# A fused attention and two expert layers on one core: second logits by column groups, both openers rearranged

## The chip, the cores and the metric

The kernel runs on one core of one Trainium2 chip, in one launch, on fp32 inputs and outputs. The metric is the device time of a run in microseconds. Before the change three runs gave 1098.56 to 1105.1, with a median of 1103.73. One execution was recorded by the hardware profiler; its own time is in the table of the section on the profile.

## The reference

Three stages run one after the other, on 3072 rows of 512 columns.

```python
# 1: attention, 4 batches x 8 heads x 768 rows x 64 columns
keep = (pos[None, :] < n_sink) | ((rel >= 0) & (rel < window))
a = softmax(where(keep, scale * q @ k.T, -1e9))
x = rows(a @ v)                                   # 3072 x 512
# 2: layer 1, 8 experts, each row goes to the expert with the largest logit
logits = x @ w_gate
out[mask] = gate_w[mask] * (relu(x[mask] @ w1[e]) @ w2[e])     # 512 -> 1024 -> 512
# 3: layer 2, the same, with a bias that depends on the row's modality
logits = x @ moe2_w_gate + modality_bias[modality_id]
out[mask] = gate_w[mask] * (relu(x[mask] @ w1[e]) @ w2[e])
```

The rows of a layer are sorted by expert on the chip, so that an expert's matmuls see its own rows alone.

## The kernel before

**Stages.** The attention takes the first 271 us: 96 units of 128 query rows of a pair of heads. While it runs, the routing of the first layer is computed for the batches that are done. Layer 1 follows as 15 blocks of 256 rows after an opener that holds block 0; layer 2 has the same form, an opener at about 714 us and 14 blocks.

**A block.** A block multiplies 256 gathered rows with one expert's `w1` (`h_products`, line 1016, TensorE tiles `hp`), keeps relu of that in a high part (`hh`, ScalarE, line 1031) and a low part (`hl`, VectorE, line 1032), and multiplies with `w2` (`y_products`, line 1025). Its second 128 rows are skipped at run time when there are none, so blocks take about 26.6 or 21.8 us. Weights come by SyncE's DMA into eight raw tiles, four of `w1` and four of `w2` (`piece`, lines 1207 and 1209); ScalarE casts each to a high part (line 1222), and VectorE or GpSimd subtracts that to get a low part (line 1225, called "low" here, numbered 0 to 7). A block prepares the weights of the next. In layer 1, lows 0 to 6 of a block are VectorE's and low 7 is GpSimd's. The rows of the next block are gathered by GpSimd (line 1230), turned by TensorE (line 1236, tiles `xp`), and split into high (line 1239, ScalarE) and low (line 1243, VectorE).

**Routing of layer 2.** Every layer-1 block also routes the rows that the block before it has put out (`Pending.route`): the rows are turned (line 1286), copied by ScalarE (line 1289), multiplied with the gate (line 1296, the "second logits"; 8 matmuls, one of 128 rows by 8 columns for each of two row tiles and four chunks of 128 columns). VectorE takes maximum and one-hot from that (lines 1325, 797 to 808), TensorE sums counts (line 817, "the prefix"), VectorE works out places and masks (lines 823 to 840), and TensorE adds them to a table (line 847).

**The openers.** Layer 1's opener (`Experts.open`) starts when the attention's last outputs are out (a branch of the instruction stream, line 742, lies between). It has the last routing of layer 1 in it, and its rows and weights are from a guess of which expert comes first. Layer 2's opener is the same code after the last routing of layer 2 (line 1366 on).

**What sets the order.** The order of each engine's instructions is fixed in the program: `Schedule.order` (line 424 on) is a list scheduler with a cost for each operation. Whenever an engine is free, it takes the ready operation with the least `late`; an operation with a larger `late` still starts when nothing else is ready on that engine. On the chip each engine works its list in order and waits for semaphores.

**Late blocks.** From layer-1 block 10 on, SyncE issues two conditional DMAs for each raw tile, one with this layer's weights and one with those of layer 2's opener (`block_load`); which of them moves data is known only at run time.

Of the kernel before, what the change touches and what calls it, by code (L numbers as in the profile page):

```python
# [74 lines left out]
class Kernel:  # L75
# [163 lines left out]
    def sink_keep(self, u):  # L239
        self.nc.gpsimd.tensor_copy(self.sp[u.pair % 2][:, u.i - 2], self.p[u.n % 4][:, :, 128:KEYS])  # L240

# [219 lines left out]
STEP = 2.05  # L461
START = {'DVE': 1.3, 'Pool': 2.0, 'SP': 9.0, 'ACT': 1.0}


class Attention:
# [20 lines left out]
    def misc(self, n):  # L486
        kk, mo, add = self.kk, self.kk.mo, lambda *args, **kw: self.add(MISC, *args, first=STEP * n, **kw)
        if n == 0:
            tmp = [("xt", 0, hp, i) for hp in range(2) for i in range(6)]
            add("DVE", 1.7, kk.masks_first, [], [("mask", 0), ("mask", 1), *tmp], late=-9)  # L490
            add("Pool", 2.8, kk.masks_window, [], [("mask", 2)], late=-9)
            add("DVE", 0.8, kk.masks_rest, [("mask", 2)], ["additive", *tmp], late=-8)
            held = [("xt", 1, hp, i) for hp in range(4) for i in range(6)]
            j = self.small()
            add("DVE", 0.4, kk.const_narrow, held, ["narrow"], late=8)
            add("DVE", 0.1, kk.mod_float, held, ["modf"], late=8)
            add("PE", 0.1, lambda: kk.mod_turn(j), [*held, "modf"], [("m", j)], late=8)
            add("DVE", 0.1, kk.mod_copy, [("m", j)], ["rowmod"], late=8)
# [14 lines left out]
    def unit(self, u):  # L513
# [7 lines left out]
        if i >= 2:  # L521
            add("Pool", 0.3, lambda: kk.sink_keep(u), [("p", n % 4)], [("sp", j, i)])
        add("PE", 0.26 * nk, lambda: kk.fast_turn(u), [("p", n % 4)], [("t", n % 2)], late=TURN_AT)
# [185 lines left out]
def attention(kk, mo, late, early):  # L709
# [147 lines left out]

OPEN_ENGINES = [["Pool", "DVE", "Pool", "Pool"] + ["Pool"] * 4, ["DVE", "Pool", "DVE", "Pool"] + ["Pool"] * 4]
OPEN_W = [2.3, 2.3]
# [7 lines left out]
class Experts:  # L867
# [124 lines left out]

    def rows_in(self, add, j, late, after=()):

        for t in range(2):
            add("PE", 0.45, lambda t=t: self.x_turn(t, t), [("xrow", t), *after], [("t", t)], late=late + 2 * PART * t)
            add("ACT", 0.55, lambda t=t: self.x_high(t), [("t", t)], ["xs", ("xh", t)], late=late + 2 * PART * t)
            add("DVE", 0.7, lambda t=t: self.x_low(t, j), [("t", t), ("xh", t), ("xrow", t)], ["xs", ("xl", t), ("rec", j)], late=late + 2 * PART * t)

# [50 lines left out]
    def open(self, router, s, then=None, w1=True, rows=True):  # L1050
# [9 lines left out]
        if rows:  # L1060
            self.rows_in(add, 0, -20)
        if not self.first:
# [22 lines left out]
    def block(self, b):  # L1085
# [127 lines left out]

    def block_load(self, m, late=False):

        ex, new, end = self.begins
        self.piece(self.w1, self.w2, ex, m, new > 0)
        if late:
            self.piece(self.io["moe2_w1"], self.io["moe2_w2"], self.opener, m, end > 0)

# [11 lines left out]

    def x_turn(self, t, turn=None):
        self.xp[t] = self.kk.bank("t", [128, 4, 128], "xp", turn)
        for c in range(4):
            self.nc.tensor.transpose(self.xp[t][:, c], self.xrow[:, t, 128 * c:128 * c + 128], self.kk.ident)  # L1236
# [23 lines left out]
class Pending:  # L1260


    def __init__(self, kk, mo):
        self.kk, self.nc, self.mo, self.yts = kk, kk.nc, mo, {}
        wk = mo.wk
        self.wg, self.yt = wk.tile([128, 4, E], F32, name="wg2"), mo.yt
# [4 lines left out]
        self.lg, self.bias, self.b, self.nmod, self.ok = f("lg", 2, E), f("bias", 2, E), f("b", 2, E), f("nmod", 2), f("ok", 2)  # L1271
        self.si = f("si", 2, dt=I32)
        self.router = Router(kk, 2, lambda *sh, dt=F32: f(f"r{next(num)}", *sh, dt=dt), "2", 1)

    def prepare(self):
        nc, io, r = self.nc, self.kk.io, self.router
        nc.sync.dma_start(self.mb, io["moe2_modality_bias"].partition_broadcast(128))
        nc.sync.dma_start(self.wg, io["moe2_w_gate"].rearrange("(c p) e -> p c e", p=128))

    def begin(self):  # L1280
        self.router.begin()

    def y_turn(self, y, t):
# [136 lines left out]
```

## Time and profile before

| | |
|---|---|
| runs: median (lowest to highest) | 1103.73 us (1098.56 to 1105.1) |
| profiled execution: its time, its span | 1100.99 us, 1098.8 us |
| mean granted TensorE clock of the profiled execution | 0.956 of full speed |
| TensorE busy | 1009.9 us, 92% |
| VectorE busy | 693.6 us, 63% |
| ScalarE busy | 551.2 us, 50% |
| GpSimd busy | 271.8 us, 25% |

The profiled execution's time and its span differ by 2.2 us, which lie outside the recorded instructions. "Busy" is the sum of an engine's instructions; an instruction that stands blocked counts as busy too. TensorE is nearly always at work in the blocks; the slices of the page in which it isn't are the first one (the start), those around 270 to 300 us (layer 1's opener), around 660 to 690 us (a late block) and around 715 to 745 us (layer 2's opener). Those four stretches, and one ordinary block, are read in the windows and timelines.

### The profile page before, as it was taken

The numbers are of one execution on the slowest core, as the hardware profiler recorded it, in microseconds if no ns is written. First come the engines' busy times: TensorE is split into PE (matmuls) and PEld (weight loads), VectorE is DVE, ScalarE is ACT, GpSimd is POOL, SyncE is SP. The second block draws the span as 40 slices with busy tenths as digits, with TensorE's granted clock in tenths as the row PEclk, the third lists the DMA queues.
The fourth block names the chain that finished last, engine by engine and source line by source line (L and its number), as shares of the span: only waits on it lengthen the run. The fifth ranks groups of instructions, "written<-read, shape, count | busy, mean of one in ns | idle before, by whom it ended". The sixth has DMA issues, their size and how long they took to land. (4 is left out here: it accounts for less than half of the span.)

```text
span 1098.8 us, 20203 instructions
## 1 busy us (share of the span) xinstructions
PE 1009.9 (92%) x6997; PEld 852.5 (78%) x6997; DVE 693.6 (63%) x1997; ACT 551.2 (50%) x1075; POOL 271.8 (25%) x269
## 2 busy tenths in 40 slices
PE   4999999987599999999999996948999999999995
PEld 2666666654499999999998995947989889898884
DVE  4565666574947877777777784664566555665554
ACT  2664656654245544445445562541555455554553
POOL 2111111113312422222223321351321112211121
PEclk9998999998599999999999997968999999999998
DMA  5355542351124142515133555211111421114610
GB/s 162 85 170 168 184 137 82 101 184 51 58 88 145 39 139 85 160 64 184 48 120 107 171 169 185 66 30 30 48 59 40 164 67 41 57 40 163 221 38 23
DMA packets 58462, 114.65 MB, mean 104 GB/s; under 512 B 10312, under 2 KB 22752, under 8 KB 58340
## 3 DMA queue, kind: packets, MB, share of 16 engines
q1 hardware_dynamic: 45860, 76.13, 20.9%
q0 software_dynamic: 11904, 36.31, 10.3%
q8 instruction: 61, 1.00, 0.4%
q10 hardware_dynamic: 576, 0.72, 0.2%
q14 instruction: 61, 0.50, 0.1%
HBM read 205.32 MB, written 28.92 MB: 213 GB/s over the span
## 5 line engine op out<-in xcount | busy, mean ns | idle before, releaser
L1025 PE MATMUL y<-w,hh 128*128 128x512 f32 x880 | 283.1, 403 | 0.0
L1225 DVE TENSOR_TENSOR w<-raw,w 128x1024 fp32r<-128x1024 f32 x161 | 192.4, 1217 | 76.0 <-ACT w L1222 75.3
L1016 PE MATMUL hp<-xs,first_w 128*128 128x256 f32 x1632 | 209.8, 285 | 1.7 <-DVE hl L1032 1.2
L1016 PEld LDWEIGHTS hp<-xs,first_w 128*128 128x128 f32 x1632 | 201.8, 191 | 6.7 <-DVE hl L1032 2.4
L1222 ACT CAST w<-raw 128x1024 fp32r<-128x1024 f32 x184 | 184.2, 1063 | 14.2 <-DMA raw<-in_moe_w_dram 11.5
L1016 PE MATMUL hp<-xs,w 128*128 128x256 f32 x1344 | 174.7, 287 | 12.3 <-DVE hl L1032 10.4
L1016 PEld LDWEIGHTS hp<-xs,w 128*128 128x128 f32 x1344 | 168.2, 193 | 16.9 <-DVE hl L1032 12.4
L1025 PEld LDWEIGHTS y<-w,hh 128*128 128x128 f32 x880 | 155.6, 189 | 25.8
L1025 PE MATMUL y<-w,hl 128*128 128x512 f32 x440 | 172.5, 392 | 0.0
L1031 ACT ACTIVATE hh<-hp 128x512 fp32r<-128x512 f32 x124 | 75.1, 606 | 131.2 <-PE hp L1016 122.7
L1225 POOL TENSOR_TENSOR w<-raw,w 128x1024 fp32r<-128x1024 f32 x23 | 60.1, 2622 | 207.8 <-ACT w L1222 207.7
L1225 DVE TENSOR_TENSOR first_w<-raw,first_w 128x1024 fp32r<-128x1024 f32 x59 | 70.3, 1220 | 64.5 <-ACT first_w L1222 64.0
L1239 ACT CAST xs<-xp 128x512 fp32r<-128x512 f32 x66 | 38.7, 586 | 142.3 <-PE xp L1236 140.5
L267 ACT ACTIVATE early<-early,late 128x272 f32<-128x272 f32 (+1 forms) x192 | 94.6, 496 | 23.4 <-DVE late L261 23.4
L1032 DVE SCALAR_TENSOR_TENSOR hl<-hp,hh 128x512 fp32r<-128x512 f32 x124 | 85.0, 686 | 30.1 <-ACT hh L1031 28.8
L261 DVE CUSTOM_DVE_ANT_0 early<-s,late 128x272 f32<-128x272 f32 (+1 forms) x192 | 72.7, 410 | 49.1 <-PE s L255 48.3
L1046 ACT ACTIVATE yrow<-y,rec 128x512 f32<-128x512 f32 x62 | 42.1, 688 | 122.0 <-PE y L1025 119.5
L1243 DVE TENSOR_TENSOR xs<-xp,xs 128x512 fp32r<-128x512 f32 x66 | 45.6, 691 | 85.7 <-ACT xs L1239 85.1
L1025 PEld LDWEIGHTS y<-w,hl 128*128 128x128 f32 x440 | 82.9, 188 | 19.1
L1256 POOL DMA_INDIRECT out_dram<-yrow,si x30 | 31.6, 1055 | 250.8 <-ACT yrow L1046 199.3
L255 PE MATMUL s<-early 64*128 64x272 f32 (+1 forms) x384 | 79.1, 444 | 11.7 <-DMA early<-in_kT_dram 9.7
L274 PE MATMUL t<-consts,early 128*128 128x128 f32 x352 | 62.4, 296 | 7.1 <-ACT early L267 4.5
(222 smaller groups left out, 1208.9 us busy)
## 6 DMA issues: line engine op xcount, KB each, us to landing
raw<-in_moe_w_dram SPq DMA_DIRECT2D x320, 512.0 KB
Y<-yrow SPq DMA_DIRECT2D x12, 514.0 KB
X<-late POOLq DMA_DIRECT2D x8, 771.0 KB, 4.5
early<-in_qT_dram SPq DMA_DIRECT2D x16, 384.0 KB
early<-in_kT_dram SPq DMA_DIRECT2D x16, 384.0 KB
early<-in_vN_dram SPq DMA_DIRECT2D x24, 256.0 KB
late<-in_vN_dram SPq DMA_DIRECT2D x64, 8.0 KB
late<-in_consts_dram ACTq DMA_DIRECT2D x1, 608.0 KB
```

The source lines that it names most:

```text
L255: self.nc.tensor.matmul(u.s[h][:, 0:u.keys], q[:, 128 * i:128 * i + 128], k.rearrange("p a s -> p (a s)")[:, KEYS * w:KEYS * w + u.keys], ...
L261: self.nc.vector.tensor_tensor_reduce(self.sc[u.n % 3][:, h, 0:n], u.s[h][:, 0:n], mask, -0.125, 3.0e38, ALU.add, ALU.min, accum_out=self. ...
L267: self.nc.scalar.activation(self.p[u.n % 4][:, h, 0:n], self.sc[u.n % 3][:, h, 0:n], AF.Exp, bias=self.nb[u.b % 2][:, u.i, g:g + 1], scale ...
L274: self.nc.tensor.transpose(u.t[:, kb, h], self.p[u.n % 4][:, h, KEYS * kb:KEYS * kb + 128], self.ident)
L1016: nc.tensor.matmul(hps[g][:, j], w[c][:, fs], xs[:, c, part], start=(c == 0 and w is whi and part == 0), stop=last)
L1025: nc.tensor.matmul(ys[t], a[:, f, ts], b[m][:, ws], start=start, stop=stop)
L1031: add("ACT", 0.6, lambda g=g, gs=gs: nc.scalar.activation(hh[:, gs], hps[g], AF.Relu), [("s", g % 2)], [("hh", g)], late=at - 3 + 2 * HALF ...
L1032: add("DVE", 0.7, lambda g=g, gs=gs: v.scalar_tensor_tensor(hl[:, gs], hps[g], 0.0, hh[:, gs].bitcast(F32), ALU.max, ALU.subtract), [("s", ...
L1046: add("ACT", 0.7, lambda t=t: nc.scalar.activation(y[:, t, 0:DM], ys[t], AF.Copy, scale=rec[:, 0, t:t + 1]), bank + ["rec"], [("out", t)], ...
L1222: self.nc.scalar.copy(self.hi[s][m], self.raw[m])
L1225: (eng or self.nc.gpsimd).tensor_tensor(self.lo[s][m], self.raw[m], self.hi[s][m].bitcast(F32), ALU.subtract)
L1243: v.tensor_tensor(self.xs[:, :, 1, t], self.xp[t], self.xs[:, :, 0, t].bitcast(F32), ALU.subtract)
```

## The change

1. **Second logits.** The 8 matmuls of `y_products` become 4 in column groups: the gate's 8 columns are the stationary side, both row tiles (256 rows) the moving side, and each chunk's result goes to its own 8 partitions (32c to 32c+7) of one bank. ScalarE copies the bank (`parts_copy`, 128 x 256), and two matmuls with a 0/1 matrix `sel` add the four groups and turn the result (`parts_sum`). The bank is cleared once, in `begin`.
2. **Openers' rows.** `rows_in` gets `early`: in the openers both turns come at once, into banks that are free there, ahead of the rest.
3. **Openers' lows.** All eight lows of each opener are VectorE's; 13 of them were GpSimd's (7 in layer 1's opener, 6 in layer 2's). Low 7 of the layer-1 blocks stays on GpSimd.
4. **Loads for the next layer.** `block_load` no longer issues the second DMA; `next_load` does, as an operation of its own with `late` 23.0 and up.
5. **Start and tail of the attention.** The masks and the first sink columns are written ahead of the branch into the fast attention instead of inside its schedule; four constants move from unit 0 to unit 10; the copies of sink columns for the last two pairs of heads (line 240) go to VectorE; the assumed start times of the engines change.

```diff
     def sink_keep(self, u):
-        self.nc.gpsimd.tensor_copy(self.sp[u.pair % 2][:, u.i - 2], self.p[u.n % 4][:, :, 128:KEYS])
+        (self.nc.vector if u.last else self.nc.gpsimd).tensor_copy(self.sp[u.pair % 2][:, u.i - 2], self.p[u.n % 4][:, :, 128:KEYS])
...
-START = {'DVE': 1.3, 'Pool': 2.0, 'SP': 9.0, 'ACT': 1.0}
+START = {'DVE': 0.5, 'Pool': 1.0, 'SP': 5.0}
...
-        if n == 0:
-            tmp = [("xt", 0, hp, i) for hp in range(2) for i in range(6)]
-            add("DVE", 1.7, kk.masks_first, [], [("mask", 0), ("mask", 1), *tmp], late=-9)
-            add("Pool", 2.8, kk.masks_window, [], [("mask", 2)], late=-9)
-            add("DVE", 0.8, kk.masks_rest, [("mask", 2)], ["additive", *tmp], late=-8)
+        if n == 10:
             held = [("xt", 1, hp, i) for hp in range(4) for i in range(6)]
...
     kk.mask_setup()
+    kk.masks_window()
+    kk.masks_first()
+    kk.masks_rest()
+    kk.k_sinks(0, nc.vector)
...
-OPEN_ENGINES = [["Pool", "DVE", "Pool", "Pool"] + ["Pool"] * 4, ["DVE", "Pool", "DVE", "Pool"] + ["Pool"] * 4]
+OPEN_ENGINES = [["DVE"] * 8] * 2
 LOW_ENGINES = [["DVE"] * 7 + ["Pool"], ["DVE"] * 8]
...
-    def rows_in(self, add, j, late, after=()):
+    def rows_in(self, add, j, late, after=(), early=False):
 
         for t in range(2):
-            add("PE", 0.45, lambda t=t: self.x_turn(t, t), [("xrow", t), *after], [("t", t)], late=late + 2 * PART * t)
...
+            keys = [("t", t)] if not early else [("o", x) for x in range(4)] if t else [("s", 2)]
+            add("PE", 0.5, lambda t=t: self.x_turn(t, early and (("o", 0) if t else ("s", 2))), [("xrow", t), *after], keys, late=late + 2 * PART * t)
...
-            self.rows_in(add, 0, -20)
+            self.rows_in(add, 0, -150, early=True)
...
-            add("SP", 0.3, lambda m=m: self.block_load(m, late), ["regs"], [("raw", m)], late=1.5 + 2.6 * m)
+            add("SP", 0.3, lambda m=m: self.block_load(m), ["regs"], [("raw", m)], late=1.5 + 2.6 * m)
+            if late:
+                add("SP", 0.3, lambda m=m: self.next_load(m), ["regs"], [("raw", m)], late=23.0 + 0.1 * m)
...
     def begin(self):
         self.router.begin()
+        self.nc.vector.memset(self.kk.bank("m", [128, 256], "lz", 2), 0.0)
...
     def y_products(self):
-        self.products = self.kk.bank("m", [128, 2, E], "lp", 2)
+
+        self.parts = self.kk.bank("m", [128, 256], "lp", 2)
+        for c in range(4):
+            self.nc.tensor.matmul(self.parts[32 * c:32 * c + E], self.wg[:, c], self.yt[:, :, 128 * c:128 * c + 128], start=True, stop=True)
+
+    def parts_copy(self):
+        self.nc.scalar.copy(self.yt[:, 0, 0:256], self.parts)
+
+    def parts_sum(self):
+        self.products = self.kk.bank("m", [128, 2, E], "lq", 2)
         for t in range(2):
-            x = grp(self.yt[:, t], 4)
-            for c in range(4):
-                self.nc.tensor.matmul(self.products[:, t], x[:, c], self.wg[:, c], start=c == 0, stop=c == 3)
+            self.nc.tensor.matmul(self.products[:, t], self.yt[:, 0, 128 * t:128 * t + 128], self.sel, start=True, stop=True)
...
-        add("PE", 1.75, self.y_products, [("yt", 0), ("yt", 1)], [("m", 2)], late=at + 3 * HALF - 0.1)
+        add("PE", 0.6, self.y_products, [("yt", 0), ("yt", 1)], [("m", 2)], late=at + 3 * HALF - 0.1)
+        add("ACT", 0.35, self.parts_copy, [("m", 2)], [("yt", 0)], late=at + 3 * HALF - 0.1)
+        add("PE", 0.45, self.parts_sum, [("yt", 0)], [("m", 2)], late=at + 3 * HALF - 0.1)
```

How this moves the instructions is shown at three places. The first is TensorE's list from the attention's end into layer 1's opener (`xn`, `lt` and `lg` are the last steps of layer 1's logits, `xp` the turned rows, `hp` the opener's first products). Before:

```order
L742 UNCONDITIONAL_BRANCH
L302 MATMUL xn<-consts,late 128x128 x4
L332 MATMUL lg<-consts,late 128x128 x3
L302 MATMUL xn<-consts,late 128x128 x8
L324 MATMUL lt<-late 32x384 x4
L817 LDWEIGHTS b_ltri
L817 MATMUL halves<-late,b_ltri 128x8
```

After the change:

```order
L742 UNCONDITIONAL_BRANCH
L1241 MATMUL xp<-consts,xrow 128x128 x8
L302 MATMUL xn<-consts,late 128x128 x4
L332 MATMUL lg<-consts,late 128x128 x3
L302 MATMUL xn<-consts,late 128x128 x8
L1017 MATMUL hp<-xs,first_w_123 128x256 x24
L324 MATMUL lt<-late 32x384 x4
```

Before, the turns and all 48 `hp` matmuls stand further down, the first `hp` behind the last table (lines 847 and 854). Now both turns stand first, and half of `hp` stands ahead of the last `lt`.

The second is VectorE's list in the middle of a layer-1 block (`raw_95` to `raw_98` are lows 3 to 6, `pd_lg` and `pd_r` the routing of layer 2, line 803 the one-hot). Before:

```order
L1032 SCALAR_TENSOR_TENSOR hl<-hp,hh 128x512
L1225 TENSOR_TENSOR w_9215<-raw_95,w_9215 128x1024
L1325 TENSOR_TENSOR pd_lg<-halves,pd_bias 128x16
L797 TENSOR_REDUCE pd_r_149<-pd_lg 128x2
L798 TENSOR_TENSOR pd_r_145<-pd_lg,pd_r_149 128x16
L1225 TENSOR_TENSOR w_9215<-raw_96,w_9215 128x1024
L800 SCALAR_TENSOR_TENSOR pd_r_148<-pd_r_145,consts 128x16
L801 TENSOR_REDUCE pd_r_150<-pd_r_148 128x2
L1225 TENSOR_TENSOR w_9215<-raw_97,w_9215 128x1024
L1032 SCALAR_TENSOR_TENSOR hl<-hp,hh 128x512
L802 TENSOR_REDUCE pd_r_151<-pd_r_146 128x2
L803 TENSOR_TENSOR pd_r_148<-consts,pd_r_150 128x16
```

After the change (lines 1229, 1033 and 1342 are what 1225, 1032 and 1325 were):

```order
L1229 TENSOR_TENSOR w_9204<-raw_96,w_9204 128x1024
L1229 TENSOR_TENSOR w_9204<-raw_97,w_9204 128x1024
L1033 SCALAR_TENSOR_TENSOR hl<-hp,hh 128x512
L1342 TENSOR_TENSOR pd_lg<-halves,pd_bias 128x16
L797 TENSOR_REDUCE pd_r_149<-pd_lg 128x2
L798 TENSOR_TENSOR pd_r_145<-pd_lg,pd_r_149 128x16
L1229 TENSOR_TENSOR w_9204<-raw_98,w_9204 128x1024
L1033 SCALAR_TENSOR_TENSOR hl<-hp,hh 128x512
L800 SCALAR_TENSOR_TENSOR pd_r_148<-pd_r_145,consts 128x16
L801 TENSOR_REDUCE pd_r_150<-pd_r_148 128x2
L802 TENSOR_REDUCE pd_r_151<-pd_r_146 128x2
L803 TENSOR_TENSOR pd_r_148<-consts,pd_r_150 128x16
```

The logits' first use has moved behind lows 4 and 5 and the second `hl`, and the steps of lines 800 to 803 behind low 6 and the third `hl`.

The third is SyncE's list at the head of a late block (`raw_92` and `raw_93` are raw tiles 0 and 1, `vi` and `gi` the experts' numbers). Before:

```order
L1152 TENSOR_LOAD vi
L1152 TENSOR_LOAD gi
L1207 ISA
L1207 DMA raw_92<-in_moe_w_dram 128x1024
L1207 ISA
L1207 DMA raw_92<-in_moe_w_dram 128x1024
L1207 ISA
L1207 DMA raw_93<-in_moe_w_dram 128x1024
```

After the change (line 1210 is what 1207 was):

```order
L1155 TENSOR_LOAD vi
L1155 TENSOR_LOAD gi
L1210 ISA
L1210 DMA raw_92<-in_moe_w_dram 128x1024
L1210 ISA
L1210 DMA raw_92<-in_moe_w_dram 128x1024
L1210 ISA
L1210 DMA raw_93<-in_moe_w_dram 128x1024
```

Each raw tile still has its two DMAs one right behind the other.

## Rows read from the trace of the kernel before

**Rows 1.** The page's busy time of each engine: us, share of the span, instructions.

```profile
PE 1009.9 (92%) x6997; PEld 852.5 (78%) x6997; DVE 693.6 (63%) x1997; ACT 551.2 (50%) x1075; POOL 271.8 (25%) x269
```

**Rows 2.** Windows: stretch, length, busy PE, PEld, DVE, ACT, POOL (instructions), PEclk, DMA.

```profile
271.10:296.60 25.50, 11.30 (x66) 7.70 (x66) 21.33 (x64) 6.19 (x11) 10.95 (x6) 0.57 0.17 64
...
296.60:321.00 24.40, 24.40 (x158) 22.27 (x157) 10.24 (x48) 4.25 (x7) 3.90 (x4) 0.96 0.16 44
...
529.40:556.00 26.60, 26.60 (x186) 24.33 (x185) 19.06 (x51) 13.37 (x19) 7.08 (x5) 1.00 0.12 41
...
653.00:693.20 40.20, 29.78 (x186) 27.12 (x187) 20.94 (x73) 13.88 (x20) 8.90 (x6) 0.83 0.61 200
...
714.40:768.30 53.90, 35.61 (x204) 32.11 (x205) 31.98 (x98) 16.20 (x23) 21.60 (x13) 0.75 0.11 30
```

**Rows 3.** Timeline, start: start, length, engine, line, operation, [idle before, releaser].

```profile
11.64 0.40 POOL L204 TENSOR_SCALAR late<-late 128x256 f32<-128x256 f32 x1
...
15.13 0.22 DVE L347 CAST late<-late 24x128 f32<-24x128 int32 x1 [1.51 <-DMA late<-in_moe_modality_id_dram]
...
16.57 0.28 DVE L261 CUSTOM_DVE_ANT_0 early<-s,late 128x128 f32<-128x128 f32 x1
```

**Rows 4.** Timeline of the attention's tail, DVE and PE.

```profile
259.76 1.18 DVE L1225 TENSOR_TENSOR first_w<-raw,first_w 128x1024 fp32r<-128x1024 f32 x1
...
263.44 0.33 PE L244 MATMUL halves<-consts,late 128*128 128x128 f32 x1 [2.42 <-POOL late L240]
```

**Rows 5.** Timeline of the first layer's opener: PE, DVE, POOL, PE.

```profile
273.38 0.63 PE L302 MATMUL xn<-consts,late 128*128 128x128 f32 x4 [2.29 <-issue]
...
281.26 5.43 DVE L825 TENSOR_TENSOR late<-late 128x24 f32<-128x24 f32 x1
...
281.98 4.65 POOL L1225 TENSOR_TENSOR w<-raw,w 128x1024 fp32r<-128x1024 f32 x2
...
295.02 1.72 PE L847 MATMUL tab<-late 128*96 128x256 bf16 x6 [3.48 <-DVE late L840]
```

**Rows 6.** Timeline of one block of the first layer: PE, POOL, DVE, PE.

```profile
534.54 1.85 PE L1296 MATMUL halves<-wg,yt 128*128 128x8 f32 x16
...
536.24 4.49 PE L1016 MATMUL hp<-xs,first_w 128*128 128x256 f32 x36
...
540.01 2.41 POOL L1225 TENSOR_TENSOR w<-raw,w 128x1024 fp32r<-128x1024 f32 x1 [13.39 <-ACT w L1222]
...
540.45 2.01 DVE L803 TENSOR_TENSOR pd_r<-consts,pd_r 128x16 f32<-128x16 f32 x1
...
544.10 0.18 PE L817 MATMUL halves<-pd_r,b_ltri 128*128 128x8 bf16 x1
...
545.03 0.62 PE L1025 MATMUL y<-w,hh 128*128 128x512 f32 x2
...
545.72 0.62 PE L1025 MATMUL y<-w,hh 128*128 128x512 f32 x2
```

**Rows 7.** Column groups in the attention (PE timeline); ACT's copies by line.

```profile
238.60 0.85 PE L324 MATMUL lt<-late 128*32 128x384 f32 x8
...
239.38 0.73 PE L255 MATMUL s<-early 64*128 64x272 f32 x4
...
L279 ACT COPY early<-t 128x256 f32<-128x256 f32 x15 | 5.6, 374 | 8.8 <-PE t L274 8.8
```

**Rows 8.** Timeline of the late blocks, SP's DMA issues and PE.

```profile
656.36 16.24 SPq L1209 DMA_DIRECT2D raw<-in_moe_w_dram  x8
...
674.93 1.44 PE L1016 MATMUL hp<-xs,w 128*128 128x256 f32 x5 [10.42 <-DVE hl L1032]
```

**Rows 9.** Timeline of the second layer's opener: POOL, DVE, PE.

```profile
736.89 6.96 POOL L1225 TENSOR_TENSOR w<-raw,w 128x1024 fp32r<-128x1024 f32 x3
...
736.19 7.69 DVE L828 TENSOR_SCALAR pd_r<-pd_r 128x2 int32<-128x2 int32 x1
...
745.15 1.21 PE L847 MATMUL tab<-pd_r,pd_r 128*96 128x256 bf16 x4 [8.24 <-DVE pd_r L840]
```

More of the change, by code (lines that the diff above doesn't have):

```diff
@@ L487, in misc @@
         kk, mo, add = self.kk, self.kk.mo, lambda *args, **kw: self.add(MISC, *args, first=STEP * n, **kw)
-        if n == 0:
-            tmp = [("xt", 0, hp, i) for hp in range(2) for i in range(6)]
-            add("DVE", 1.7, kk.masks_first, [], [("mask", 0), ("mask", 1), *tmp], late=-9)
-            add("Pool", 2.8, kk.masks_window, [], [("mask", 2)], late=-9)
-            add("DVE", 0.8, kk.masks_rest, [("mask", 2)], ["additive", *tmp], late=-8)
+        if n == 10:
             held = [("xt", 1, hp, i) for hp in range(4) for i in range(6)]
             j = self.small()
[L495 to L498, printed above, removed]
+            add("DVE", 0.4, kk.const_narrow, held, ["narrow"])
+            add("DVE", 0.1, kk.mod_float, held, ["modf"])
+            add("PE", 0.1, lambda: kk.mod_turn(j), [*held, "modf"], [("m", j)])
+            add("DVE", 0.1, kk.mod_copy, [("m", j)], ["rowmod"])
         if n == 14:
@@ L521, in unit @@
         if i >= 2:
-            add("Pool", 0.3, lambda: kk.sink_keep(u), [("p", n % 4)], [("sp", j, i)])
+            add("DVE" if u.last else "Pool", 0.25, lambda: kk.sink_keep(u), [("p", n % 4)], [("sp", j, i)])
         add("PE", 0.26 * nk, lambda: kk.fast_turn(u), [("p", n % 4)], [("t", n % 2)], late=TURN_AT)
@@ L617, in all @@
             u.b, u.hp = divmod(pair, H // 2)
+            u.last = pair >= pairs - 2
             u.i, u.n, u.pair, u.keys, u.copy = i, n, pair, WIDE if i else 128, "DVE" if COPY_DVE(n) else "ACT"
@@ L723, in attention @@
         kk.k_load(n)
-    kk.k_sinks(0, nc.vector)
     kk.wg1, kk.mod = late.take(4, 32), late.take(TILES)
@@ L991, in weights_in @@
         add(eng, 2.5 if eng == "Pool" else 1.27, lambda: self.low(s, m, self.nc.vector if eng == "DVE" else None), [("raw", m), ("hi", m)], [("lo", m), *reads], late=late, **kw)
-    def rows_in(self, add, j, late, after=()):
+    def rows_in(self, add, j, late, after=(), early=False):
         for t in range(2):
-            add("PE", 0.45, lambda t=t: self.x_turn(t, t), [("xrow", t), *after], [("t", t)], late=late + 2 * PART * t)
-            add("ACT", 0.55, lambda t=t: self.x_high(t), [("t", t)], ["xs", ("xh", t)], late=late + 2 * PART * t)
-            add("DVE", 0.7, lambda t=t: self.x_low(t, j), [("t", t), ("xh", t), ("xrow", t)], ["xs", ("xl", t), ("rec", j)], late=late + 2 * PART * t)
+            keys = [("t", t)] if not early else [("o", x) for x in range(4)] if t else [("s", 2)]
+            add("PE", 0.5, lambda t=t: self.x_turn(t, early and (("o", 0) if t else ("s", 2))), [("xrow", t), *after], keys, late=late + 2 * PART * t)
+            add("ACT", 0.55, lambda t=t: self.x_high(t), keys, ["xs", ("xh", t)], late=late + 2 * PART * t)
+            add("DVE", 0.7, lambda t=t: self.x_low(t, j), [*keys, ("xh", t), ("xrow", t)], ["xs", ("xl", t), ("rec", j)], late=late + 2 * PART * t)
     def rows_fetch(self, add, rows, late, reads=()):
@@ L1212, in block_registers, with block_load, next_load @@
         self.begins = self.load(self.vi[0:1, b], E - 1, engines=(mybir.EngineType.SP,))
[L1214 to L1219, printed above, removed]
+    def block_load(self, m):
+        self.piece(self.w1, self.w2, self.begins[0], m, self.begins[1] > 0)
+    def next_load(self, m):
+        self.piece(self.io["moe2_w1"], self.io["moe2_w2"], self.opener, m, self.begins[2] > 0)
     def high(self, s, m):
@@ L1231, in gather, with x_turn @@
                                               in_offset=bass.IndirectOffsetOnAxis(ap=rows[:, t:t + 1], axis=0))
-    def x_turn(self, t, turn=None):
-        self.xp[t] = self.kk.bank("t", [128, 4, 128], "xp", turn)
+    def x_turn(self, t, bank=None):
+        kind, turn = bank or ("t", t)
+        self.xp[t] = self.kk.bank(kind, [128, 4, 128], "xp", turn)
         for c in range(4):
@@ L1265, in __init__ @@
         wk = mo.wk
-        self.wg, self.yt = wk.tile([128, 4, E], F32, name="wg2"), mo.yt
+        self.wg, self.sel, self.yt = wk.tile([128, 4, E], F32, name="wg2"), wk.tile([128, E], F32, name="sel"), mo.yt
         self.mb = wk.tile([128, 2, E], F32, name="mb")
@@ L1270, in __init__ @@
         self.pay, self.pi = f("pay", 2, 2), f("pi", 2, 2, dt=I32)
-        self.lg, self.bias, self.b, self.nmod, self.ok = f("lg", 2, E), f("bias", 2, E), f("b", 2, E), f("nmod", 2), f("ok", 2)
+        self.lg, self.bias, self.nmod, self.ok = f("lg", 2, E), f("bias", 2, E), f("nmod", 2), f("ok", 2)
         self.si = f("si", 2, dt=I32)
         self.router = Router(kk, 2, lambda *sh, dt=F32: f(f"r{next(num)}", *sh, dt=dt), "2", 1)
+        self.b = self.router.b
     def prepare(self):
@@ L1278, in prepare @@
         nc.sync.dma_start(self.wg, io["moe2_w_gate"].rearrange("(c p) e -> p c e", p=128))
+        nc.vector.tensor_reduce(self.sel, self.kk.ident.rearrange("p (c e) -> p e c", c=4)[:, 0:E], AX.X, ALU.add)
     def begin(self):
         self.router.begin()
+        self.nc.vector.memset(self.kk.bank("m", [128, 256], "lz", 2), 0.0)
     def y_turn(self, y, t):
```

## The prediction

> **What bounds the kernel.** I read the page's busy times first. TensorE is busy for 1009.9 us, 92% of the span [rows 1], so about 89 us are not TensorE's work, and a change that takes little work off it can win only where it waits. The windows show where. An ordinary layer-1 block is full: TensorE is busy for 26.60 of 26.60 us [rows 2]. Layer 1's opener is not: between the attention's end at 271.1 and 296.6 TensorE works 11.30 of 25.50 us, while VectorE shows 21.33 and GpSimd 10.95; the stretch from 296.6 to 321.0 is full again [rows 2]. Layer 2's opener has 35.61 of 53.90, and one late block takes 40.20 us with 29.78 of work [rows 2]. The chain of waits reaches back only over the last blocks and tells nothing of these places, so I went on with the timelines of each.
>
> In the openers the reader is to see VectorE's tiny instructions stand for microseconds beside GpSimd's subtractions: line 825 (128x24) takes 5.43 us and ends when the two lows on GpSimd end, at 281.98 + 4.65 = 286.63 [rows 5]; line 828 (128x2) takes 7.69 beside three lows of 6.96 [rows 9]. They feed the masks, and TensorE waits 3.48 and 8.24 us for masks ahead of its tables [rows 5, 9].
>
> **Start.** The masks on GpSimd end at 11.64 + 0.40 = 12.04, but the first score on VectorE starts at 16.57 [rows 3]; between lies, among others, a cast that waited 1.51 us for the modality DMA [rows 3] and now comes ten units later. With the masks done ahead of the branch I put the first score at about 14: three small mask steps behind 12.04 and the read of the branch's flag. Gain 2.5; bounds 0 (if a load ends last) and 2.9.
>
> **Tail of the attention.** TensorE waits 2.42 us for GpSimd's copy of line 240, which stood behind two gathers [rows 4]. On VectorE it has two new lows of 1.18 ahead of it [rows 4], so the wait becomes 1.6 at worst: gain 0.8; bounds 0 and 2.4.
>
> **Layer 1's opener.** From 271.1 to the next block at 321.0 are 49.9 us, with 11.30 + 24.40 = 35.7 of TensorE's work [rows 2]. The branch's 2.29 [rows 5] stays, so 38.0 is the floor and 11.9 the most that can go. The turns now stand first and 24 `hp` ahead of the last logits, so products fill the waits of the routing. VectorE gets four lows, 4 x 1.18 = 4.7, but loses the blocked time of line 825 alone, 5.43 less some 0.2. What becomes late next is the gather of the next block's rows: it follows the last table, and fewer products are left behind the table to cover it. I allow 3 for that wait with its turn and copies, and take 9. Least: 5, line 825's time alone.
>
> **Layer-1 blocks.** The second logits' 16 records stand from 534.54 to the next product at 536.24, 1.70 us [rows 6]. Nearest to the column groups is line 324, 8 records of 384 columns, 238.60 to 239.38, 0.78 us [rows 7]; for 256 columns 0.52, between 0.26 (a third) and 0.78. The two sums are 4 records of the old kind, 4/16 of 1.70 = 0.43. Saving 1.70 - 0.95 = 0.75 a block, between 0.49 and 1.01.
>
> But the saving has to get past the prefix. The new ScalarE copy, 0.37 [rows 7], stands among the casts, the logits reach VectorE behind two more lows, and lines 800 to 803 stand behind low 6 and the third `hl`. TensorE started the prefix at 544.10 [rows 6]; it now comes 0.75 earlier but has one more step of `y` ahead of it, 545.72 - 545.03 = 0.69 [rows 6], so it asks at 544.04. When is the one-hot there? Line 803 waited in this block until GpSimd's low 7 ended (540.01 + 2.41 = 542.42; line 803 ended at 542.46) [rows 6]. With the copy low 7 can start at about 540.4. If VectorE's low 6 goes first (1.18, from about 540.2), GpSimd follows until 543.8, and six small steps of some 0.1 follow: 544.5, a wait of 0.46. If GpSimd goes first, 542.8 + low 6 + the third `hl` + the same steps give 545.3, a wait of 1.26. Without the change TensorE would have come to the same point at 544.10 + 0.69 = 544.79. So a block gains 0.3 or loses 0.5. I take 0.2, nearer to the first, since low 6's input is ready first. Ahead of the late blocks' wait a saving only lengthens that wait, so I count 12 of 15: 2.4.
>
> The Trainium skill ("SBUF — State Buffer", Who interferes with whom) says that a VectorE instruction with two SBUF inputs and a GpSimd instruction that reads SBUF exclude each other for a whole instruction, and that the one issued first blocks the other. By that rule alone the blocks give 12 x 0.3 = 3.6 and the sum falls by 1.2. The trace agrees in line 803; it disagrees in line 825, which was issued at 281.26, 0.72 ahead of GpSimd's lows, and lost all the same [rows 5].
>
> **Layer 2's opener.** The 8.24 us ahead of its tables [rows 9] are there because three lows on GpSimd held line 828; those lows are VectorE's now and none is left on GpSimd. VectorE was busy 31.98 of 53.90 us [rows 2], 7.5 of it blocked in line 828, so six lows of 1.18 (7.1) fit in their place. Gain 8.2; bounds 5 (the lows stand ahead of the masks) and 11 (some of the other idle of 53.90 - 35.61 = 18.3 goes too).
>
> **Loads for the next layer.** In the late blocks SyncE's 8 issues take 16.24 us, and TensorE waits 10.42 in the block from 653 [rows 8], which is 40.20 long where 26.60 is full [rows 2]. The change means to part the two loads of a raw tile, yet SyncE's list still has them in pairs: the second becomes ready right behind the first on an idle queue, and a larger `late` doesn't hold it back. So 0.
>
> **Sum.** 2.5 + 0.8 + 9 + 2.4 + 8.2 = 22.9 off the profiled execution's 1100.99 gives 1078.1. That execution is 2.7 below the runs' median of 1103.73, from which the sum gives 1080.8. I take 1079.
>
> **Rivals.**
>
> The logits' saving arrives in full, because VectorE keeps up and the prefix never waits: 12 x 0.75 = 9.0 instead of 2.4, 1072. For it: VectorE was busy only 19.06 of 26.60 us in a block [rows 2]. Against it: the chain above. Chance 0.15.
>
> GpSimd's low 7 goes first in every block: -0.5 x 12 = -6 instead of +2.4, 1087. For it: line 825 lost though issued first. Chance 0.14.
>
> The column groups don't overlap, so that the logits save nothing; then TensorE asks for the prefix at 544.8, waits 0 to 0.5, and the blocks give 0 to -6: 1081 to 1087. The row speaks against it: 8 records of 384 columns pass in 0.78, the switch into the groups and out of them included [rows 7]. Chance 0.05. The Trainium skill ("TensorEngine Tiling (Array Packing)", Key Properties) says that a change of tiling mode drains TensorE, which would take from the saving; the row has such a drain inside its 0.78 if there is one.
>
> VectorE becomes the bound in the openers: the lows stand ahead of the masks and the gains halve to 8.6 of 17.2: 1088. For it: 21.33 of 25.50 busy [rows 2]; against it: much of that was blocked time. Chance 0.13.
>
> The loads do come apart at run time, or the earlier start of their chain frees the late block: 40.20 - 26.60 = 13.6 more, 1065. Against it stands SyncE's list. Chance 0.06.
>
> On the other side: in every layer-1 block the prefix waits so long that it eats the rest, 20.5 us in 12 blocks, 1.7 each. That needs the one-hot at 544.79 + 1.7 = 546.5, when GpSimd is first and ScalarE's copy and casts come one cast later still; from 547.4 on (2.6 a block) the kernel is over 1% slower, 1112. Against it: two delays must meet in all blocks. Chance 0.04, half of it beyond 1%.
>
> The forecast keeps 0.43. The range takes in its own bounds and the rivals except the far ends: 1064 to 1091. About 1%, 11 us, is what a measurement of this kernel tells from no change. Faster by over that means below 1093 and holds in all cases but the last and the worst of the openers' and blocks' losses together: 0.89. Within it 0.09, slower 0.02.
>
> **What would show it.** In the changed kernel's profile: the first score near 14 us; no VectorE instruction of over 2 us in either opener and no GpSimd low there; `hp` of layer 1's opener within 12 us of the attention's end, and the next block some 41 us after it with a wait of 1 to 3 us for gathered rows; about 0.8 us less of wait at line 244; a second-logits group of about 0.5 us with sums of 0.4, and a wait of 0.4 to 1.3 at the prefix; no wait over 1 us ahead of layer 2's tables; a late block that still waits about 10 us for a load. I would be wrong first in the openers, if the gather chain after the last table is longer than the products that are left, or in the blocks, if the order of low 6 and low 7 goes the other way.

## The result and the profile after

The changed kernel takes 1072.38 us (median of four runs, 1070.82 to 1073.76) against 1103.91 (four runs, 1098.56 to 1105.1): a ratio of 0.9723, 95% interval 0.9688 to 0.9758. The forecast was 1079 with a range of 1064 to 1091. The profiled execution took 1072.99, 28.0 less than the one before.

The page's busy times answer to [rows 1]: TensorE works 16.5 us less, and GpSimd 34.

```profile
PE 993.4 (93%) x6933; PEld 823.2 (77%) x6933; DVE 688.9 (64%) x2020; ACT 555.6 (52%) x1091; POOL 237.9 (22%) x248
```

The windows answer to [rows 2] (stretch, length, busy PE, PEld, DVE, ACT, POOL, then PEclk, DMA share, GB/s): layer 1's opener up to the next block, one full block, a late block, and layer 2's opener up to the next block.

```profile
272.07:310.15 38.08, 31.80 (x222) 27.60 (x222) 26.06 (x106) 11.90 (x21) 3.61 (x4) 0.96 0.16 57
...
514.55:540.75 26.20, 26.20 (x183) 23.01 (x182) 18.87 (x51) 13.65 (x20) 7.35 (x5) 1.00 0.13 41
...
637.10:677.20 40.10, 29.90 (x181) 26.23 (x182) 20.91 (x73) 14.03 (x21) 8.29 (x7) 0.87 0.63 206
...
697.88:740.68 42.80, 30.76 (x199) 26.01 (x200) 26.52 (x101) 16.31 (x24) 8.78 (x7) 0.88 0.13 40
```

The reader is to see four lengths: 38.08 where 49.9 stood, 26.20 where 26.60 stood, 40.10 where 40.20 stood, and 42.80 where 53.90 stood. Full blocks took 26.60 and 26.74 in turn before, 26.67 on average, so one gains 0.47. The attention's end, however, is at 272.07 instead of 271.09. From these the difference of the two spans, 27.6, adds up: -1.0 to the attention's end, +11.8 in the first opener, +11.1 in the second, and +5.7 between the two, in layer 1's blocks.

The start and the attention, TensorE but for the first row and GpSimd's two (line 171 puts sink columns into the keys, line 240 keeps sink columns, and line 244 turns what line 240 has kept):

```profile
14.32 0.27 DVE L261 CUSTOM_DVE_ANT_0 early<-s,late 128x128 f32<-128x128 f32 x1
...
44.03 0.26 POOL L171 COPY early<-early 128x80 f32<-128x80 f32 x1 [4.12 <-PE t L274]
...
44.23 0.21 POOL L240 COPY late<-early 128x32 f32<-128x32 f32 x1
...
29.07 0.27 PE L244 MATMUL halves<-consts,late 128*128 128x128 f32 x1
...
44.49 0.33 PE L244 MATMUL halves<-consts,late 128*128 128x128 f32 x1 [0.60 <-POOL late L240]
...
49.61 0.49 PE L285 MATMUL o<-late 128*128 128x128 f32 x2 [0.50 <-ACT late L295]
...
54.63 0.48 PE L255 MATMUL s<-early 64*128 64x128 f32 x2 [0.43 <-DVE late L261]
...
56.79 0.27 PE L244 MATMUL halves<-consts,late 128*128 128x128 f32 x1
...
250.69 0.66 PE L274 MATMUL t<-consts,early 128*128 128x128 f32 x4 [2.71 <-DVE late L318]
...
263.57 0.47 PE L244 MATMUL halves<-consts,late 128*128 128x128 f32 x1 [0.64 <-DVE late L240]
...
274.22 1.06 PE L1241 MATMUL xp<-consts,xrow 128*128 128x128 f32 x8 [2.15 <-issue]
```

The first score comes 2.25 us earlier than in [rows 3], and the first of the halves steps (line 244) at 29.07 came at 29.55 before. Then waits follow, and the third halves step is at 56.79. The wait of [rows 4] at line 244 is 0.64 now, but 2.71 stand ahead of a turn at 250.69.

Layer 1's opener, TensorE, to the next block:

```profile
279.60 4.83 PE L1017 MATMUL hp<-xs,first_w 128*128 128x256 f32 x24
...
307.34 1.04 PE L1241 MATMUL xp<-consts,xrow 128*128 128x128 f32 x8
...
309.25 0.39 PE L1017 MATMUL hp<-xs,first_w 128*128 128x256 f32 x1 [0.87 <-ACT xs L1244]
...
310.15 1.57 PE L1017 MATMUL hp<-xs,first_w 128*128 128x256 f32 x11 [0.52 <-DVE xs L1248]
```

The first products start 7.5 us after the attention's end. Behind the last `y` stand the turns of the next block's rows and waits of 0.87 and 0.52: the exposed gather.

One layer-1 block, TensorE, VectorE and GpSimd, as in [rows 6]:

```profile
519.79 0.62 PE L1303 MATMUL halves<-yt,wg 128*8 128x256 f32 x8
...
520.34 3.06 PE L1017 MATMUL hp<-xs,first_w 128*128 128x256 f32 x24
...
523.24 0.51 PE L1311 MATMUL halves<-sel,yt 128*128 128x8 f32 x4
...
523.60 1.65 PE L1017 MATMUL hp<-xs,first_w 128*128 128x256 f32 x12
...
529.43 0.17 PE L817 MATMUL halves<-pd_r,b_ltri 128*128 128x8 bf16 x1
...
525.33 3.39 POOL L1229 TENSOR_TENSOR w<-raw,w 128x1024 fp32r<-128x1024 f32 x1 [13.27 <-ACT w L1226]
...
525.23 1.22 DVE L1229 TENSOR_TENSOR w<-raw,w 128x1024 fp32r<-128x1024 f32 x1
...
526.97 1.78 DVE L800 SCALAR_TENSOR_TENSOR pd_r<-pd_r,consts 128x16 f32<-128x16 f32 x1
...
529.20 0.18 DVE L807 TENSOR_TENSOR pd_r<-pd_r,pd_ok 128x16 bf16<-128x16 f32 x1
```

The column groups take 520.34 - 519.79 = 0.55, the sums 0.36. Low 7 was issued 0.1 behind low 6, shows 3.39 instead of 2.41, and holds line 800 for 1.78. The one-hot (line 807, which starts at 529.20) is just in time: TensorE's step of `y` would have let it go on at about 529.28, and it starts the prefix at 529.43.

A late block (ScalarE, TensorE) and layer 2's opener (TensorE):

```profile
658.68 1.99 ACT L1226 CAST w<-raw 128x1024 fp32r<-128x1024 f32 x2 [6.39 <-DMA raw<-in_moe_w_dram]
...
664.92 0.17 PE L817 MATMUL halves<-pd_r,b_ltri 128*128 128x8 bf16 x1 [6.66 <-DVE pd_r L807]
...
707.29 1.11 PE L1241 MATMUL xp<-consts,xrow 128*128 128x128 f32 x4 [3.98 <-DMA xrow<-Y,ri]
...
725.51 0.87 PE L847 MATMUL tab<-pd_r,pd_r 128*96 128x256 bf16 x4
```

A late block still waits: ScalarE's cast waits 6.39 us for a load, the `hh`, the `hl` and line 800 stand behind it, and so TensorE waits 6.66 us for the one-hot. All its waits in this block make 40.10 - 29.90 = 10.2 us, where 40.20 - 29.78 = 10.4 stood. Ahead of layer 2's tables, where 8.24 stood in [rows 9], there is no wait.

### The profile page after: what moved, and what is told of

Same layout as the page of the kernel before. It is cut to its first block, busy times and chain, and to the rows that moved or that the text cites. A ratio compares the mean times of both kernels' runs of the same rounds, so it can differ in the third digit from the quotient of the medians.

```text
span 1071.2 us, 19987 instructions
## 1 busy us (share of the span) xinstructions
PE 993.4 (93%) x6933; PEld 823.2 (77%) x6933; DVE 688.9 (64%) x2020; ACT 555.6 (52%) x1091; POOL 237.9 (22%) x248
## 5 line engine op out<-in xcount | busy, mean ns | idle before, releaser
L1229 DVE TENSOR_TENSOR w<-raw,w 128x1024 fp32r<-128x1024 f32 x169 | 201.0, 1219 | 71.2 <-ACT w L1226 70.2
L1017 PEld LDWEIGHTS hp<-xs,first_w 128*128 128x128 f32 x1632 | 199.4, 189 | 13.3 <-issue 3.5
L1229 DVE TENSOR_TENSOR first_w<-raw,first_w 128x1024 fp32r<-128x1024 f32 x64 | 76.2, 1220 | 67.4 <-ACT first_w L1226 66.8
L1229 POOL TENSOR_TENSOR w<-raw,w 128x1024 fp32r<-128x1024 f32 x15 | 46.4, 3091 | 198.3 <-ACT w L1226 184.4
```

What stands on the lines that cost most here:

```text
L1017: nc.tensor.matmul(hps[g][:, j], w[c][:, fs], xs[:, c, part], start=(c == 0 and w is whi and part == 0), stop=last)
L1229: (eng or self.nc.gpsimd).tensor_tensor(self.lo[s][m], self.raw[m], self.hi[s][m].bitcast(F32), ALU.subtract)
```

## The experiments

Each is compared with the changed kernel's 1072.38; where a stage of one execution says more than the run, the stage is given.

**The start and the attention as before.** Part 5 of the change undone:

```diff
-START = {'DVE': 0.5, 'Pool': 1.0, 'SP': 5.0}
+START = {'DVE': 1.3, 'Pool': 2.0, 'SP': 9.0, 'ACT': 1.0}
...
-        if n == 10:
+        if n == 0:
+            add("DVE", 1.7, kk.masks_first, [], [("mask", 0), ("mask", 1), *tmp], late=-9)
...
```

> The changed kernel with its start and attention as before the change (masks inside the schedule, constants at unit 0, line 240's last copies on GpSimd, the old start values); openers, logits and loads as changed. If the start and the tail are worth the 3.3 us that the prediction gave them, this run is 1075.7 against the changed kernel's 1072.4. If the attention gave that back inside, as its end at 272.07 in the changed kernel against 271.09 before suggests, this run is 1.0 faster, 1071.4, and the attention ends at 271.1.

Measured: 1071.28 (1069.46 to 1075.8). Part 5 is worth nothing that can be told. The attention ended at 269.27:

```profile
272.17 1.20 PE L1242 MATMUL xp<-consts,xrow 128*128 128x128 f32 x8 [2.90 <-issue]
```

(272.17 - 2.90). With the changed attention it ended between 268.89 and 272.07 in seven profiles, so the changed kernel's own 272.07 is the late end of a spread of 3 us, and the step from 271.09 to 272.07 is no result. One thing more shows here and in the next run. The wait of [rows 4] ahead of line 244 is 0.22 in this run, with the copies of line 240 on GpSimd and the lows on VectorE; and the next run, with the copies on VectorE and the lows back on GpSimd, has none:

```profile
261.30 0.33 PE L244 MATMUL halves<-consts,late 128*128 128x128 f32 x1 [0.22 <-POOL late L240]
...
261.69 0.45 PE L244 MATMUL halves<-consts,late 128*128 128x128 f32 x1
```

So either move takes most of that wait away by itself. (In this run TensorE also comes to it later, after 2.19 us for ScalarE, line 267, where 1.24 stand in the changed kernel.)

**The openers' lows back on GpSimd.**

```diff
-OPEN_ENGINES = [["DVE"] * 8] * 2
+OPEN_ENGINES = [["Pool", "DVE", "Pool", "Pool"] + ["Pool"] * 4, ["DVE", "Pool", "DVE", "Pool"] + ["Pool"] * 4]
```

> The changed kernel with the 13 lows of the openers back on GpSimd; the early turns stay. If GpSimd's subtractions, which hold VectorE's small instructions, are what the openers paid for, most of the 23.6 us that the two openers gained is lost: about 16 us slower, 1088, with VectorE instructions of several us beside GpSimd's lows. If the early turns alone carry the gain, this run is within 4 us of the changed kernel, 1072 to 1076.

Measured: 1089.39 (1087.05 to 1092.51), 17.0 slower, as expected (the expectation's 23.6 for the two openers is 22.9 by the windows above). Most of the loss is in layer 2's opener; GpSimd, VectorE, GpSimd and TensorE there:

```profile
727.45 1.01 POOL L1261 DMA_INDIRECT Y<-yrow,pd_si  x1 [0.17 <-issue]
...
727.89 7.56 DVE L831 SCALAR_TENSOR_TENSOR pd_r<-pd_r,pd_r 128x2 f32<-128x2 f32 x1
...
728.48 6.94 POOL L1229 TENSOR_TENSOR w<-raw,w 128x1024 fp32r<-128x1024 f32 x3
...
736.25 0.59 PE L847 MATMUL tab<-pd_r,pd_r 128*96 128x256 bf16 x2 [7.18 <-DVE pd_r L840]
```

A step of 128x2 elements stands for 7.56 us beside three lows, and TensorE waits 7.18 for the masks, as in [rows 9]. From the end of layer 1's work to the next block's products are 56.4 us against 42.8. In layer 1's opener (attention's end to the next block's full products) it is 40.6 against 38.1.

**The openers' turns late.**

```diff
-            self.rows_in(add, 0, -150, early=True)
+            self.rows_in(add, 0, -20)
```

> The changed kernel with the openers' turns where they were (own banks, late -20); the lows stay on VectorE. If the lows are the larger part, this run is some 3 us slower, 1075, since the first products wait for the turns for a few us and the routing no longer stalls. If the early turns are the larger part, it is 12 or more slower, 1084 or above.

Measured: 1078.59 (1076.55 to 1084.21), 6.2 slower, between the two values expected. Here the loss is in layer 1's opener, 45.8 against 38.1, and only 0.6 in layer 2's. The window of that opener, and two rows of TensorE in it:

```profile
268.90:314.70 45.80, 36.63 (x221) 30.71 (x222) 28.07 (x116) 10.37 (x18) 5.49 (x6) 0.78 0.18 59
...
287.71 1.72 PE L847 MATMUL tab<-late 128*96 128x256 bf16 x6 [4.04 <-DVE late L840]
...
289.29 9.09 PE L1017 MATMUL hp<-xs,first_w 128*128 128x256 f32 x60
```

The first products come behind the tables again, after a wait of 4.04, and the same work takes 36.63 us of TensorE at a granted clock of 0.78, where the changed kernel needs 31.80 at 0.96.

**The old second logits.**

```diff
-        self.parts = self.kk.bank("m", [128, 256], "lp", 2)
+        self.products = self.kk.bank("m", [128, 2, E], "lp", 2)
...
-        add("ACT", 0.35, self.parts_copy, [("m", 2)], [("yt", 0)], late=at + 3 * HALF - 0.1)
-        add("PE", 0.45, self.parts_sum, [("yt", 0)], [("m", 2)], late=at + 3 * HALF - 0.1)
```

> The changed kernel with the second logits as before (8 matmuls of 128 x 8, no copy, no sum). The changed kernel's layer-1 blocks are 26.20 us where 26.60 stood before. If the column groups saved that, blocks are 26.6 again and the run is 4 to 5 us slower, 1077. If the order and the lows around them saved it, the blocks stay below 26.4 and the run is within 2 us. In the changed kernel a step of y takes 0.700 us in layer 1 and 0.687 before; if the column groups do that, the step is 0.687 here.

Measured: 1081.17 (1080.31 to 1084.78), 8.8 slower, twice what was expected. A full block is 26.67:

```profile
518.98:545.65 26.67, 26.67 (x187) 24.29 (x186) 18.99 (x53) 13.36 (x20) 7.10 (x5) 1.00 0.13 41
```

So the column groups save 0.47 in a full block. From the first products of the block behind layer 1's opener to the end of layer 1's work it is 396.8 us against 388.6, and layer 2's opener is 44.7 against 42.8. The step of `y` (three matmuls of 512 columns) is 0.700 here too, so the column groups don't slow it.

**The loads apart.**

```diff
-            if late:
-                add("SP", 0.3, lambda m=m: self.next_load(m), ["regs"], [("raw", m)], late=23.0 + 0.1 * m)
+        for m in range(8 if late else 0):
+            add("SP", 0.3, lambda m=m: self.next_load(m), ["regs"] + [("raw", x) for x in range(m, 8)], [("raw", m)], late=23.0 + 0.1 * m)
```

> The changed kernel, but each load for the next layer's opener now depends on all eight loads of the block, so that SyncE's list has the eight block loads first and the eight others behind them. If the pairs, of which the second waits for the first to land, make the late blocks' stall (TensorE waits 6.66, 1.85, 1.69 and 1.69 us there in the changed kernel), the stall goes and the run is 8 to 11 us faster, 1062 to 1064. If the stall is the bytes' own time (DMA share 0.61 in that stretch), nothing changes: 1071 to 1074.

Measured: 1062.04 (1060.85 to 1064.68), 10.3 faster; ratio to the kernel before 0.9634 (0.9595 to 0.9674). SyncE's issues in one late block (start, time, count):

```profile
639.73 4.99 SPq L1210 DMA_DIRECT2D raw<-in_moe_w_dram  x4
...
645.79 7.51 SPq L1212 DMA_DIRECT2D raw<-in_moe_w_dram  x4
...
653.62 2.39 SPq L1210 DMA_DIRECT2D raw<-in_moe_w_dram  x4
...
656.22 3.32 SPq L1212 DMA_DIRECT2D raw<-in_moe_w_dram  x4
```

The sixteen issues take 20 us in all, with a pause in them, where [rows 8] had 16.24 for eight. In the late block SyncE waits 18.1 us for loads of raw tiles to land in the changed kernel, and not at all here. The largest wait of TensorE in the late blocks is 2.23 us; the late block takes 31.09 where 40.10 stood and the one ahead of it 21.14 where 22.86 stood, while the one behind it takes 23.1 for 20.7. The rest of the 10.3 is not placed: the two attentions alone end 2.1 us apart.

**The constants yield, at unit 10.**

```diff
-            add("DVE", 0.4, kk.const_narrow, held, ["narrow"])
+            add("DVE", 0.4, kk.const_narrow, held, ["narrow"], late=8)
```

> The changed kernel with the four constants still at unit 10 but with late 8, so that VectorE does its score work first when both are ready. If the constants, 0.7 us of VectorE at 38.7 us, are what lost the lead of the start between 40 and 55 us (1.9 us), the attention ends about 1.9 us earlier, at 270.2, and the run is 1070.5. If the lost lead is due to the other moves in the attention's order, nothing changes: 1072.

Measured: 1072.14 (1071.94 to 1079.78): no gain. From the first to the third halves step it is 28.4 us, against 27.7 in the changed kernel and 25.66 before. TensorE waits 1.22 us at the second halves step, for line 240's copy at 42.66, which stands behind line 171 at 42.46. That VectorE does the constants ahead of scores is not the cause.

**Low 7 on VectorE in the layer-1 blocks.**

```diff
-LOW_ENGINES = [["DVE"] * 7 + ["Pool"], ["DVE"] * 8]
+LOW_ENGINES = [["DVE"] * 8, ["DVE"] * 8]
```

> The changed kernel with low 7 of the layer-1 blocks on VectorE as well, so that no GpSimd subtraction is left beside VectorE's small steps. In the changed kernel line 800 stands 1.78 us beside low 7, and the one-hot comes 0.15 us after TensorE asks for it. If that blocked time bounds the blocks, 15 blocks gain 0.15 to 0.3 each: 1068 to 1070. If VectorE's 1.2 us more per block come late for the products, the run is slower by up to 0.5 a block, 1080. If neither, 1072.

Measured: 1073.30 (1071.61 to 1074.02): the same. A full block takes 26.07 against 26.20, so the blocked time of line 800 costs it 0.13 at most. But the second block takes 21.7 against 20.9, with a wait of 1.03 us for the next rows (ScalarE, line 1244), and the late block 42.3 against 40.1, and over the whole of layer 1 the gain is gone. What makes those blocks longer was not followed up.

**The constants at unit 2.**

```diff
-        if n == 10:
+        if n == 2:
...
-            add("DVE", 0.4, kk.const_narrow, held, ["narrow"])
+            add("DVE", 0.4, kk.const_narrow, held, ["narrow"], late=8)
```

> The changed kernel with the four constants at unit 2 and late 8; TensorE's and GpSimd's lists between the first and the third halves step (line 244) are then as before the change, with the masks still ahead of the branch. In six profiles of the changed attention this stretch took 27.5 to 27.8 us, in two of the old one 25.66. If the order at unit 10 lost the lead of the start, the stretch is 25.7 here, and the run is about 2 us faster than the changed kernel, 1070.4. If the constants cost the same wherever they stand, it is 27.6 and 1072.4.

Measured: 1070.16 (1067.98 to 1072.53). The difference of 2.2 is what was expected, but the runs overlap, and those with the old attention (1071.28) overlap too; the stretch alone can be told. GpSimd and TensorE:

```profile
39.90 0.21 POOL L240 COPY late<-early 128x32 f32<-128x32 f32 x1 [0.80 <-ACT early L267]
...
43.26 0.26 POOL L171 COPY early<-early 128x80 f32<-128x80 f32 x1 [3.16 <-DMA early<-in_kT_dram]
...
28.25 0.27 PE L244 MATMUL halves<-consts,late 128*128 128x128 f32 x1
...
53.91 0.27 PE L244 MATMUL halves<-consts,late 128*128 128x128 f32 x1
```

25.66 us, as before the change, and no wait over 0.25 for TensorE in it. In this stretch TensorE's and ScalarE's instructions come in the same order as before the change; with the constants at unit 10 the order of all four engines is another. One thing that follows can be named. Here the third copy of line 240 (39.90) comes ahead of line 171, which waits for the keys' DMA until 43.26. In the changed kernel it stands behind line 171 (44.23 behind 44.03), as in the run with yielding constants, and TensorE's line 244 waits for it.

**The addresses as before.** The change also drops a small tile of the second routing (`pd_b`), and the tiles behind it moved. Here the 0/1 matrix is put into its space:

```diff
-        self.wg, self.sel, self.yt = wk.tile([128, 4, E], F32, name="wg2"), wk.tile([128, E], F32, name="sel"), mo.yt
+        self.wg, self.yt = wk.tile([128, 4, E], F32, name="wg2"), mo.yt
...
+        self.slot = f("b", 2, E)
+        self.sel = self.slot[:, 0]
```

> The changed kernel with the 0/1 matrix of the sums placed in the space of the routing tile that the change dropped, so that every tile behind has its old address. A step of y in layer 1 takes 0.700 us in the changed kernel and in the run with the old logits, 0.687 before. If the shifted addresses make that, the step is 0.687 here and the 15 blocks gain about 0.2 each: 1069.4. If not, 0.700 and 1072.4.

Measured: 1072.30 (1068.47 to 1077.51). The step of `y` is 0.688, as before the change, but a block is 26.13 against 26.20, worth 1 us in 15 blocks, which the run can't tell.

**Combined**, the loads apart and the constants at unit 2 together:

> The changed kernel with the loads apart and the constants at unit 2 with late 8. If the two add, about 10.3 us from the loads and 2 from the constants: 1060. If the constants are worth nothing, 1062.

Measured: 1058.82 (1058.2 to 1062.58); ratio to the kernel before 0.9614 (0.9578 to 0.965). It beats both kernels, by 13.6 the changed one.

**Combined, with the old addresses and low 7 on VectorE:**

> The combined kernel (loads apart, constants at unit 2) with the old addresses and with low 7 of the layer-1 blocks on VectorE. If the step of y is 0.687 and no GpSimd subtraction holds the one-hot, so that TensorE no longer waits at the prefix, 15 blocks gain 0.2 to 0.35 each over the combined kernel's 1058.8: 1054 to 1056. If either is taken back elsewhere in the block, as with the old addresses alone, 1058 to 1059.

Measured: 1060.28 (1058.22 to 1061.43): nothing more. Most full blocks take 26.04 to 26.17, and the second block 21.8 against 20.9, as in the run with low 7 on VectorE.

## Why the prediction was right, and where it was not

- **The sum.** It gave 22.9 us off the profiled execution, and 28.0 were measured. Of the 27.6 between the spans, start and tail make -1.0 where I gave 3.3, the openers 22.9 where I gave 17.2, and the blocks 5.7 where I gave 2.4. The first miss offsets part of the two others, so that 1079 came as near as it did is in part luck.
- **Start and tail: the step that failed.** I gave them 2.5 and 0.8; the first experiment shows neither a gain nor a loss, within about 2 us. The first score did come at 14.3, and the first halves step of seven profiles of the changed attention came 0.5 to 1.8 us earlier than 29.55. That lead is not the start's alone: the step came at 27.14 to 29.54 in the four other profiles with the new start, whose orders up to there differ only by the constants, and it goes with the moment at which TensorE's clock rose (see the last section). What lead there was went before the third step: 27.5 to 27.8 us in all seven against 25.66. My sum named the move of the constants from unit 0 to unit 10 and gave it no price, because I had not followed it into the order of the engines. With the constants at unit 2 the 25.66 are back, in three profiles. Of the 2.06 us, waits of 0.60, 0.50 and 0.43 are named in the profile; the first is for the copy behind line 171, and what the other two follow from was not tried by itself.
- **The tail's wait** at line 244 shrank by more than forecast, 2.42 to 0.64, but by the first two experiments the move of line 240 and that of the lows each do it alone; and 2.71 us ahead of a turn at 250.69, for line 318, took the place of the 0.46 that stood there.
- **Layer 1's opener: right in kind, 11.8 for 9.** The exposed gather was sized well (allowed 3; the turns and two waits make 2.4). The floor of 38.0 was met, 38.08, but was not one: waits of 2.71, 0.87 and 0.52 are still in it. It took the 35.7 us of TensorE's work as fixed, though 11.30 of it ran at a granted clock of 0.57 [rows 2]. With the waits filled the whole stretch runs at 0.96 and the work is 31.80. My reading that line 825's block is the least to be gained was the wrong way round: undone one at a time, the early turns carry 7.7 of the 11.8 and the lows 2.5, and with the turns late the lows gain 49.9 - 45.8 = 4.1, less than the 5 that I called the least.
- **Layer 2's opener: right, 11.1 for 8.2.** The 8.24 ahead of the tables is gone, and the lows do it: 13.6 are lost without them, and with the turns late the opener is 43.4, still 10.5 shorter than before. Missing in the sum were the second logits here, 1.9, and the turns, 0.6.
- **The blocks: the mechanism right, the size 0.47 for 0.2.** Logits and sums cost 0.91 (forecast 0.95). VectorE's low 6 went ahead of low 7, as taken. Put on the old block's times (14.87 later), TensorE asked for the prefix at 544.15 (forecast 544.04) and the one-hot was there at 544.25 (544.5), so the wait was 0.15, not 0.46. Low 7 ended at 543.59 instead of 543.8, and the steps behind it were a little shorter.
- **Who holds whom.** In the changed block the instruction that started first won: low 6 (525.23) held low 7 (525.33), and that held line 800. The Trainium skill ("SBUF — State Buffer", Who interferes with whom) has that rule, and these rows agree. In the openers VectorE started first and lost: line 825 at 281.26 to the low at 281.98 [rows 5], line 828 at 736.19 to that at 736.89 [rows 9], and line 831 at 727.89 to that at 728.48 with the lows back on GpSimd. Each time GpSimd was then on the issue of a DMA that stands directly ahead of its low (two of the three below); whether that issue is what held VectorE, no run shows. The twelve products ahead of the logits now take 1.63 us until the groups start, 1.50 before. If that 0.13 is the drain that the Trainium skill ("TensorEngine Tiling (Array Packing)", Key Properties) names, it is small against the 0.79 that the groups save.

```profile
281.14 0.83 POOL L361 DMA_DIRECT2D X<-late  x1 [1.11 <-DVE late L357]
...
735.87 1.02 POOL L1256 DMA_INDIRECT Y<-yrow,pd_si  x1 [0.17 <-issue]
```

- **The loads: right that nothing moves**, 40.10 for 40.20. That the pairs make the stall was an inference from the order; the loads apart show it, by the late block's 31.09 and a run that is 10.3 us faster.
- **The rivals.** The full saving (1072) has the measured time but not its reason: 0.47 a block, not 0.75. VectorE as the bound of the openers, GpSimd first, and groups that don't overlap are each refuted by the rows above.

## What to carry over

A delay taken out at the head of a list is worth what the list leaves of it, so compare the order of every engine over the stretch that follows, also those that the edit doesn't name. Where an engine's work stands at a low granted clock, its busy time is no floor: filling the waits shortens the work too. A due time in a greedy scheduler doesn't hold an operation back; a dependency does.

## What was not expected of the hardware

TensorE's first scores take 0.32 us each (1.28 for four) and later 0.18. The windows print a granted clock of 1.00 over the first 98 us, but the trace's record of the clock begins only at 27.08 us in the changed kernel, and that is where the rate changes; the 1.00 ahead of it stands for no record. Four scores take 1.28 again at 101.79, in a stretch with a recorded clock of 0.50, so the first scores ran at the lower of the clock's two levels, 1.2 GHz, and the later ones at 2.4. TensorE had been at work without a pause from about 14.4 on. Rows of the changed kernel, TensorE, and the window of the third:

```profile
24.25 1.28 PE L255 MATMUL s<-early 64*128 64x272 f32 x4
...
29.27 0.73 PE L255 MATMUL s<-early 64*128 64x272 f32 x4
...
101.79 1.28 PE L255 MATMUL s<-early 64*128 64x272 f32 x4
...
98.76:105.58 6.82, 6.25 (x28) 4.65 (x30) 4.29 (x19) 2.39 (x10) 0.44 (x2) 0.50 0.42 157
```

The record begins at 22.03 to 27.08 us in the eleven profiles with the new start, and at 25.58 and 27.20 in the two with the old one. The start's gain is worth less the later the clock rises: with the constants at unit 2 the first halves step is at 27.45 where the clock rose at 22.03, and at 29.54, no earlier than before the change, where it rose at 26.62.

A step of `y` takes 0.700 or 0.688 us with nothing changed but the addresses of tiles.
